# Finished projection chains scaled by ScalarE and added by GpSimd in place of VectorE, in a one-core attention and Fourier kernel

## The chip, the core and the metric

The kernel runs on one core of a Trainium2 chip. The core has a matmul engine (TensorE, "PE" in the profile; its weight loads stand apart as "PEld"), VectorE ("DVE"), ScalarE ("ACT"), GpSimd ("POOL") and SyncE ("SP"), which here only issues DMAs. Each engine takes its instructions from a queue of its own, in the order in which the program wrote them. The metric is the device time of one execution in microseconds (us); lower is better.

## The reference

```
g = sigmoid(sum(x * gate_w))                       # one gate per row
a = Real(DFT_seq(DFT_hid(x)))                      # Cr @ (x @ Wr) - Ci @ (x @ Wi)
qkv = x @ wqkv ; 32 heads of 16                    # attention over the same x
p = softmax(q @ k^T / 4)
b = (p @ v, heads side by side) @ wo
out = g * a + (1 - g) * b                          # 2048 x 512, fp32
```

There are 2048 rows and 512 columns. All products that need more accuracy are split into a high and a low part and taken three times (high x high, high x low, low x high).

## The kernel before, in words

**Stages.** First come the projections to q, k and v, the imaginary half of the hidden DFT and the gate. The long middle part runs attention and, woven into it, the Fourier products. Its unit of work is a "unit": one pair of heads, one key tile of 128, and a half (1024) of the queries. There are 16 pairs x 32 units = 512 (`UNITS`). Each unit has four score products (`scores`, L721, exponentiated by ScalarE in L722 into `pt`) and its value products (`pv`, L757). The maxima that the softmax needs are made ahead from a second set of score products (`a_tile`, L222), which VectorE reduces (L224). When the maxima of half of a head pair are complete, `m_parts` (VectorE L233, GpSimd L236 and L237) and `m_rows` (VectorE L241, then four DMAs from SP and four from GpSimd, L245) write them as two extra rows into the query stack `qs`; SP writes those of head 0, GpSimd those of head 1. The scores of that half read them.

**Sections.** `segment` writes one section by hand: score products on one half of TensorE's rows, products of some accumulating chain on the other, and at the bar `|` the value products of two units. Two sections make a pair that handles the upper and lower halves of the contraction for the same chain products. The pattern `FULL` carries 16 chain products (the Fourier chains over the sequence), the pattern `NINE` carries nine, which is one whole chain of the output projection:

```
NINE = "aS s a s a sA a a s a s sA |", "aS a s s a sA a s a s s aS sA |"
for gen, n in ((proj(1, (0, 1, 2), one), 8), (first, 6)):
    for i in range(n):
        yield NINE, take(gen, 9)
```

So there are 14 pairs of `NINE` sections, for row tiles 8 to 15 and then 0 to 5. They begin at value step 432 and end at step 488. The chain (`Chain`) lies in a PSUM bank of its own (`psD`, tile name `d`). The scores, maxima and value products share the seven other banks, each taken by `bank`, which picks the one that its clocks expect to be free first.

**The end of a section.** At the bar, `segment` writes in this order: the finishes of chains that ended there (`late`, which calls `proj_next` and `finish`), then `add_sums` (the GpSimd add L772 of the value products of the section before, whose copy `oe` ScalarE made in L766 into one of two buffers; the first group of a half is copied straight into `osum`, L763), then `run_plan` (work that falls due at a value step), then the value products of this section, then one deferred step of the maxima.

**Due at the end.** `run_plan` puts the last column block of the attention output into step 486 (`last_block` step 0: two GpSimd memsets L533 and twelve loads by SP, L539 and L540, into `o_raw`), into step 490 (the GpSimd product L574) and into step 494 (VectorE, L562 and L563). Behind step 488 come eleven steps written out in `whole`, in which the last chains run on all rows of TensorE, and then the last pair of heads (`LastPair`, `last_pair`).

**A finish.** `finish` adds `(1 - g)` times a chain to the row tile `yp[t]`. Its VectorE form is one instruction (L596). It also has a form with ScalarE and GpSimd (L593, L594), which only three finishes at the very end use, with the tile `few` for the scaled chain.

Of the kernel before, what the change touches and what calls it, by code (L numbers as in the profile page):

```python
# [9 lines left out]
F32 = mybir.dt.float32  # L10
# [5 lines left out]
P = 128  # L16
S = 2048
D = 512
# [5 lines left out]
UNITS = NP * 32  # L24
# [7 lines left out]
def mix_kernel(ctx: ExitStack, tc: tile.TileContext, xa_t, xa, wqkv, w_hid, w_seq, wo, gate_w, out):  # L32
# [317 lines left out]
    work = ctx.enter_context(tc.tile_pool(name="work", bufs=1, side="right", reuse_waits="tile"))  # L350
# [134 lines left out]
    oh, yp, wos = {}, {}, []  # L485
# [101 lines left out]
    few, by_others = [], set()  # L587

    def finish(ps, t, y, other=False):
        if other:  # L590

            tmp = few[0][:, t % 4]
            nc.scalar.activation(tmp, ps, AF.Copy, scale=omg[:, t:t + 1])  # L593
            nc.gpsimd.tensor_tensor(y, y, tmp, ALU.add)  # L594
            return
        nc.vector.scalar_tensor_tensor(y, ps, omg[:, t:t + 1], y, op0=ALU.mult, op1=ALU.add)  # L596

    def proj(hf, cts, pools):

        for qt in range(8):  # L600
            t = hf * 8 + qt
            chain = Chain(pools[qt % len(pools)], 3 * len(cts))
            for ct in cts:
                h1, l1 = oh[hf, ct][qt]
                for i, (st, mv) in enumerate(((h1, 0), (h1, 1), (l1, 0))):
                    last = ct == cts[-1] and i == 2
                    yield chain, st, wos[0][:, mv, ct], partial(proj_next, hf, cts, t, chain) if last else None

    def proj_next(hf, cts, t, chain):
        finish(chain.ps, t, yp[t], t in by_others)  # L610
        if hf == 0 and cts[-1] == 3:
            nc.sync.dma_start(out[t * P:(t + 1) * P, :], yp[t])

# [23 lines left out]
    class LastPair:  # L637
# [31 lines left out]
        def products(self, others):  # L669

            pss = [o_bank() for _ in range(4)]
            for i, (st, mv) in enumerate(((0, 0), (0, 1), (1, 0))):
                for c in range(4):
                    r = slice(32 * c, 32 * c + 32)
                    nc.tensor.matmul(pss[c], self.o15[r, st], w15[0][r, mv], start=i == 0, stop=i == 2)  # L675
            for c in range(4):
                t = 8 + 4 * self.blk + c
                y = yp.pop(t)
                finish(pss[c], t, y, c in others)
                nc.sync.dma_start(out[t * P:(t + 1) * P, :], y)  # L680
# [185 lines left out]
    users, valued = [], 0  # L866
# [159 lines left out]
```

## Time and profile before

| what | us |
|---|---|
| median of 3 runs (lowest, highest) | 1688.51 (1687.78, 1689.23) |
| the profiled execution | 1688.01 |
| its span on the core | 1686.2 |
| busy: PE, DVE, ACT, POOL | 1674.4, 1370.7, 1246.6, 747.8 |
| one finish on VectorE (L596), median of those from bank `d` | 0.74 |
| one scaling on ScalarE (L593) / one add on GpSimd (L594) | 0.69 / 1.27 |

Matmuls are pipelined and their ends are modelled, so a PE that is busy all the time still has waits inside; they show as idle time ahead of a weight load (PEld), with the engine that ended it. In a timeline row stand the start, the time, the engine, the source line, the operation, the tiles (out<-in), the shape, the count, and in brackets the idle time of that engine before it and what ended it. "SPq" is SyncE's DMA queue.

### The profile page before, as it was taken

The numbers are of one execution on the slowest core, as the hardware profiler recorded it, in microseconds if no ns is written. First come the engines' busy times: TensorE is split into PE (matmuls) and PEld (weight loads), VectorE is DVE, ScalarE is ACT, GpSimd is POOL, SyncE is SP. The second block draws the span as 40 slices with busy tenths as digits, with TensorE's granted clock in tenths as the row PEclk, the third lists the DMA queues.
The fourth block names the chain that finished last, engine by engine and source line by source line (L and its number), as shares of the span: only waits on it lengthen the run. The fifth ranks groups of instructions, "written<-read, shape, count | busy, mean of one in ns | idle before, by whom it ended". The sixth has DMA issues, their size and how long they took to land.

```text
span 1686.2 us, 34488 instructions
## 1 busy us (share of the span) xinstructions
PE 1674.4 (99%) x13072; PEld 1016.5 (60%) x13072; DVE 1370.7 (81%) x2283; ACT 1246.6 (74%) x2472; POOL 747.8 (44%) x807
## 2 busy tenths in 40 slices
PE   9999999999999999999999999999999999999998
PEld 7888766655555555555555555555555555565643
DVE  5448688888888888888888888888888888899944
ACT  5212288887777888777777788778777888787896
POOL 0114634554444465444444466445554465322230
PEclk9999999999999999999999999999999999999999
DMA  9963500314141533314155533332241536740114
GB/s 295 340 151 114 174 10 21 45 51 77 44 83 46 102 97 83 70 46 95 45 132 189 103 121 86 86 68 60 70 89 46 112 96 129 263 70 8 33 27 139
DMA packets 82486, 165.15 MB, mean 98 GB/s; under 512 B 19777, under 2 KB 20033, under 8 KB 78481
## 3 DMA queue, kind: packets, MB, share of 16 engines
q1 hardware_dynamic: 77968, 162.56, 37.3%
q8 instruction: 103, 1.69, 0.5%
q0 software_dynamic: 4352, 0.39, 0.3%
q14 instruction: 63, 0.51, 0.1%
HBM read 107.73 MB, written 54.52 MB: 96 GB/s over the span
## 4 chain that ended last, share of the span: by engine, by line
PE 98%; POOL 1%; DMA 0%; issue 0%; DVE 0%; ACT 0%; DVEq 0%; POOLq 0%; ACTq 0%
PE d L416 38%; PE t L757 27%; PE t L222 12%; PE t L721 8%; PE t L315 4%; PE t L89 2%; PE t L90 2%; PE t L88 2%; PE t L333 1%; PE t L738 1%; PE t L416 0%; DMA raw<-wqkv 0%; POOL hl L292 0%; PE t L675 0%; DMA b<-hl 0%
## 5 line engine op out<-in xcount | busy, mean ns | idle before, releaser
L224 DVE TENSOR_REDUCE mx<-t 128x1 f32<-128x512 f32 x2022 | 1253.9, 683 | 197.6 <-PE t L222 153.1
L722 ACT ACTIVATE pt<-t 128x512 f32<-128x512 f32 x2048 | 1035.1, 629 | 9.5 <-PE t L721 9.3
L721 PE MATMUL t<-qs,ks 50*128 50x512 f32 x2048 | 737.5, 411 | 0.6 <-ACT y L432 0.5
L222 PE MATMUL t<-ks,qs 48*128 48x512 f32 x2022 | 689.9, 400 | 0.0
L416 PE MATMUL d<-xab,ch 64*128 64x512 f32 x2016 | 656.9, 400 | 0.0
L757 PE MATMUL t<-pt,vt 128*32 128x512 f32 x3968 | 477.5, 598 | 0.0
L416 PEld LDWEIGHTS d<-xab,ch 64*128 64x128 f32 x2016 | 357.8, 184 | 132.5 <-issue 99.8
L222 PEld LDWEIGHTS t<-ks,qs 48*128 48x128 f32 x2022 | 366.4, 185 | 91.1 <-ACT pt L722 37.4
L721 PEld LDWEIGHTS t<-qs,ks 50*128 50x128 f32 x2048 | 366.8, 185 | 75.3 <-DVE mx L224 34.9
L416 PE MATMUL d<-xab,cl 64*128 64x512 f32 x1008 | 403.8, 401 | 0.0
L772 POOL TENSOR_TENSOR osum<-osum,oe 128x512 f32<-128x512 f32 x217 | 280.1, 1291 | 164.8 <-ACT oe L766 157.4
L766 ACT COPY oe<-t 128x512 f32<-128x512 f32 x217 | 127.7, 589 | 236.1 <-PE t L757 234.3
L757 PEld LDWEIGHTS t<-pt,vt 128*32 128x32 f32 x3968 | 105.0, 109 | 229.6 <-issue 148.7
L371 POOL CAST ch<-craw 128x512 fp32r<-128x512 f32 x126 | 77.4, 615 | 349.8 <-PE t L721 305.2
L416 PEld LDWEIGHTS d<-xab,cl 64*128 64x128 f32 x1008 | 185.7, 184 | 68.2 <-issue 51.1
L372 POOL TENSOR_TENSOR cl<-craw,ch 128x512 fp32r<-128x512 f32 x126 | 162.6, 1290 | 10.2
L245 POOL DMA_DIRECT2D qs<-mt x128 | 72.3, 570 | 81.9 <-DVE mt L241 75.3
L416 PE MATMUL d<-wo_hl,o_hl 64*128 64x512 f32 (+1 forms) x270 | 72.6, 392 | 0.8 <-DVE yp_qs L596 0.8
L416 PE MATMUL d<-wre,xab 64*128 64x512 f32 x288 | 70.4, 389 | 0.0
L416 PEld LDWEIGHTS d<-wre,xab 64*128 64x128 f32 x288 | 52.9, 185 | 3.8 <-DVE mx L224 0.3
L416 PEld LDWEIGHTS d<-wo_hl,o_hl 64*128 64x128 f32 (+1 forms) x270 | 49.5, 185 | 4.8 <-DVE yp_qs L596 1.3
L89 PE MATMUL t<-xab,wh 128*128 128x512 f32 x128 | 49.9, 390 | 0.2 <-DVE xab L85 0.2
(121 smaller groups left out, 893.3 us busy)
## 6 DMA issues: line engine op xcount, KB each, us to landing
craw<-w_seq SPq DMA_DIRECT2D x128, 256.0 KB
qk<-hl SPq DMA_DIRECT2D x32, 512.0 KB
qs<-qk SPq DMA_DIRECT2D x96, 128.0 KB
ks<-qk SPq DMA_DIRECT2D x96, 128.0 KB
b<-hl SPq DMA_DIRECT2D x16, 512.0 KB
xab<-b SPq DMA_DIRECT2D x16, 512.0 KB
o<-osum SPq DMA_DIRECT2D x62, 128.0 KB
oh<-nh SPq DMA_DIRECT2D x12, 512.0 KB
```

The lines of the kernel that those rows point to most:

```text
L89: nc.tensor.matmul(ps, sh, ml, start=False, stop=False)
L222: nc.tensor.matmul(ps, qs[p % 2][r, qt * P:(qt + 1) * P], ks[p % 2][r, kb * 512:(kb + 1) * 512], start=True, stop=True)
L224: user = nc.vector.tensor_reduce(mx[p % 2][:, h, qt, kb:kb + 1], ps, AX.X, ALU.max)
L245: (nc.sync, nc.gpsimd)[h].dma_start(rows.rearrange("v (q b c) -> v b q c", q=8, b=4)[:, b], mt[hf][32 * b + h:32 * b + 32:2])
L371: nc.gpsimd.tensor_copy(h1, raw)
L372: nc.gpsimd.tensor_tensor(l1, raw, h1.bitcast(F32), ALU.subtract)
L416: i = nc.tensor.matmul(self.ps, st[r], mv[r], start=not self.begun, stop=stop)
L721: nc.tensor.matmul(ps, ks[p % 2][rr, kt * P:(kt + 1) * P], qs[p % 2][rr, q0:q0 + 512], start=True, stop=True)
L722: return nc.scalar.activation(pts[u][:, 2 * qb + h], ps, AF.Exp, bias=0.0, scale=DH ** -0.5)
L757: nc.tensor.matmul(acc[32 * j:32 * j + 32], vt[:, kt, p, h:h + 32], pt[:, j], start=u == us[0], stop=u == us[-1])
L766: nc.scalar.copy(oe, acc)
L772: nc.gpsimd.tensor_tensor(o, o, oe, ALU.add)
```

## The change

In all 14 pairs of `NINE` sections, `finish` takes its second form: ScalarE scales the chain out of its bank into a tile in SBUF, and GpSimd adds that tile to the row tile. The condition `valued < UNITS - 24` is true for every value step below 488. The tile `few` does not exist yet at that time, so the scaled chain goes into two tiles of the working pool in turn, `nh` for even row tiles and `no` for odd ones. Both served the column blocks of the attention output before and are used again at step 494. Finishes behind step 488 stay as they were. The patterns of the sections and the choice of the banks are not touched.

```
     def finish(ps, t, y, other=False):
         if other:
-            tmp = few[0][:, t % 4]
+            tmp = few[0][:, t % 4] if few else work.tile([P, 2, D], F32, name="no" if t % 2 else "nh")[:, 0]
             nc.scalar.activation(tmp, ps, AF.Copy, scale=omg[:, t:t + 1])
             nc.gpsimd.tensor_tensor(y, y, tmp, ALU.add)
             return
         nc.vector.scalar_tensor_tensor(y, ps, omg[:, t:t + 1], y, op0=ALU.mult, op1=ALU.add)
...
     def proj_next(hf, cts, t, chain):
-        finish(chain.ps, t, yp[t], t in by_others)
+        finish(chain.ps, t, yp[t], t in by_others or valued < UNITS - 24)
         if hf == 0 and cts[-1] == 3:
             nc.sync.dma_start(out[t * P:(t + 1) * P, :], yp[t])
```

More of the change, by code (lines that the diff above doesn't have):

```diff
@@ L590, in finish @@
         if other:
-            tmp = few[0][:, t % 4]
+            tmp = few[0][:, t % 4] if few else work.tile([P, 2, D], F32, name="no" if t % 2 else "nh")[:, 0]
             nc.scalar.activation(tmp, ps, AF.Copy, scale=omg[:, t:t + 1])
@@ L609, in proj_next @@
     def proj_next(hf, cts, t, chain):
-        finish(chain.ps, t, yp[t], t in by_others)
+        finish(chain.ps, t, yp[t], t in by_others or valued < UNITS - 24)
         if hf == 0 and cts[-1] == 3:
```

## The prediction, made before the changed kernel ran

> **What bounds the kernel now.** I read the page, then the windows of the stage that the change touches, then the timeline of each engine there and after it.
>
> ```profile
> PE 1674.4 (99%) x13072; PEld 1016.5 (60%) x13072; DVE 1370.7 (81%) x2283; ACT 1246.6 (74%) x2472; POOL 747.8 (44%) x807
> ...
> core 0: us, PE busy (x) PEld busy (x) DVE busy (x) ACT busy (x) POOL busy (x), PEclk, DMA share, GB/s
> 1513.70:1525.00 11.30, 11.30 (x86) 6.63 (x82) 10.40 (x19) 9.03 (x18) 2.58 (x2) 1.00 0.21 79
> ```
>
> TensorE never goes empty, and the sections with nine products ("nine sections") come in pairs of 11.30 us. In one pair VectorE works 10.40, ScalarE 9.03, GpSimd 2.58. So VectorE looks nearly full, and whether taking 0.74 from it helps depends on where that 0.74 lies. This is one pair end, in order of time (the all-engine timeline):
>
> ```profile
> 1508.36 0.18 PEld L222 LDWEIGHTS t<-ks,qs 48*128 48x128 f32 x1 [0.84 <-DVE mx L224]
> 1508.89 4.88 DVE L224 TENSOR_REDUCE mx<-t 128x1 f32<-128x512 f32 x8 [0.47 <-PE t L721]
> 1508.98 4.52 ACT L722 ACTIVATE pt<-t 128x512 f32<-128x512 f32 x9
> 1512.45 1.92 PE L757 MATMUL t<-pt,vt 128*32 128x512 f32 x16
> 1513.68 0.74 DVE L596 SCALAR_TENSOR_TENSOR yp<-d,omg,yp 128x512 f32<-128x512 f32 x1
> 1514.30 0.18 PEld L222 LDWEIGHTS t<-ks,qs 48*128 48x128 f32 x1 [0.84 <-DVE mx L224]
> 1514.48 0.18 PEld L416 LDWEIGHTS d<-wo_hl,o_hl 64*128 64x128 f32 x1
> 1514.52 0.59 ACT L766 COPY oe<-t 128x512 f32<-128x512 f32 x1 [1.02 <-PE t L757]
> 1514.84 4.88 DVE L224 TENSOR_REDUCE mx<-t 128x1 f32<-128x512 f32 x8 [0.42 <-PE t L721]
> ```
>
> While TensorE does the value products (from 1512.45) it hands VectorE nothing new. The finish (L596) runs there, and afterwards VectorE is still idle for 0.42 us until TensorE's next score. In the half without a finish (1508.89) that idle time is 0.47, and the restart of TensorE shows the same 0.84 at 1508.36 and 1514.30. So the finish is hidden already: its removal lengthens an idle stretch and is worth 0.
>
> **The change, part by part.** 14 finishes lie in the nine sections (8 of the second half's rows, 6 of the first's). Each loses one VectorE instruction of 0.74 and gains a ScalarE scaling and a GpSimd add. TensorE's instructions keep their order, and the choice among the seven banks is what it was.
>
> *ScalarE.* The same form already runs once, at the end of a long chain just ahead of these sections (timelines of ScalarE and GpSimd):
>
> ```profile
> 1452.16 0.59 ACT L766 COPY oe<-t 128x512 f32<-128x512 f32 x1 [1.29 <-PE t L757]
> 1452.64 4.03 ACT L722 ACTIVATE pt<-t 128x512 f32<-128x512 f32 x8
> 1456.56 0.69 ACT L472 ACTIVATE y<-d,ng 128x512 f32<-128x512 f32 x1
> 1457.97 0.59 ACT L766 COPY oe<-t 128x512 f32<-128x512 f32 x1 [0.72 <-PE t L757]
> 1457.32 1.29 POOL L473 TENSOR_TENSOR y<-y,yr 128x512 f32<-128x512 f32 x1 [8.94 <-ACT y L472]
> 1458.56 2.66 POOL L772 TENSOR_TENSOR osum<-osum,oe 128x512 f32<-128x512 f32 x2
> ```
>
> A scaling of 0.69 between the exponentials and the copy of the value products shrank ScalarE's idle time from 1.29 to 0.72 and moved nothing else. In a nine section it has 1.02 to fit into, so about 0.4 is left: cost 0. Without that cover it would be 14 x 0.69 = 9.7. Queued behind it on ScalarE is only that copy. The bank of the chain comes free at 1508.98 + 4.52 + 0.6 = 1514.1, not at 1514.42, and TensorE loads for its next use at 1514.48: no gain there either, since the matmuls beside it set that time.
>
> *GpSimd.* 14 adds of 1.29 (L473) on an engine that is busy 2.58 of 11.30: room enough. What changes is its order. The queue is in program order, the add of a finish is put ahead of the add of the first half's value products (L772), and it waits for ScalarE's end of the section. So that L772, which ran at once, runs up to 6 us later. In most pairs nobody needs it: it is done by 1514.1 + 0.07 + 1.24 + 1.29 = 1516.7, and its buffer (one of two) is wanted by the copy of the next section's products, a half pair of 5.35 after 1514.52, at 1519.9. The last pair differs, because more hangs behind it in the same queue:
>
> ```profile
> 1611.04 1.30 POOL L772 TENSOR_TENSOR osum<-osum,oe 128x512 f32<-128x512 f32 x1 [4.10 <-ACT oe L766]
> 1612.25 1.87 POOL L533 MEMSET o_raw<- 128x1024 f32 x2
> 1615.38 0.20 POOL L236 CAST nhl<-nm 128x16 fp32r<-128x16 f32 x1 [1.26 <-DVE nm L233]
> 1622.79 2.38 POOL L574 TENSOR_TENSOR o_raw<-o_raw 128x1024 f32<-128x1024 f32 x1 [4.83 <-DMA o_raw<-r]
> 1625.11 2.31 POOL L245 DMA_DIRECT2D qs<-mt  x4
> 1627.44 3.07 POOL L772 TENSOR_TENSOR osum<-osum,oe 128x512 f32<-128x512 f32 x2
> ...
> 1613.26 0.51 SPq L539 DMA_DIRECT2D o_raw<-o  x1
> ...
> 1620.39 0.59 SPq L540 DMA_DIRECT2D o_raw<-r  x1
> 1621.08 2.75 SPq L245 DMA_DIRECT2D qs<-mt  x4
> ```
>
> The memsets (L533) gate twelve loads that SP issues without a pause from 1613.26 to 1621; behind these stand SP's four writes of the maxima rows (L245); GpSimd's L574 waits for the last load, and GpSimd's own four L245 wait behind L574. In the changed order the add of row tile 5 stands ahead of L772 and the memsets. When does it run?
>
> ```profile
> 1610.80 4.52 ACT L722 ACTIVATE pt<-t 128x512 f32<-128x512 f32 x9
> 1616.02 0.59 ACT L766 COPY oe<-t 128x512 f32<-128x512 f32 x1 [0.70 <-PE t L757]
> ...
> 1632.53 0.59 ACT L766 COPY oe<-t 128x512 f32<-128x512 f32 x1
> 1633.01 4.03 ACT L722 ACTIVATE pt<-t 128x512 f32<-128x512 f32 x8
> ...
> 1632.34 1.82 PE L721 MATMUL t<-qs,ks 50*128 50x512 f32 x8
> 1634.16 1.92 PE L757 MATMUL t<-pt,vt 128*32 128x512 f32 x16
> ...
> DMA to landing us min/median/max: 1.7/1.7/2.1
> ```
>
> The exponentials end at 1615.32. L472 began 0.11 before its group's end, so the scaling runs 1615.21 to 1615.90 and the copy at 1616.02 is not moved. The add follows 0.07 later (1457.25 to 1457.32): 1615.97. One such add passes to the next in 1.24 (1457.32 to 1458.56), L772 to the memset in 1.21 (1611.04 to 1612.25): the memset starts at 1618.42 in place of 1612.25, **6.17 late**. Everything in the two queues that I named moves by this: SP's L245 end at 1623.83 + 6.17 = 1630.0, GpSimd's last L245 is issued at 1627.42 - 0.58 + 6.17 = 1633.0, and with 1.7 to landing its rows are there at 1634.7.
>
> Who needs them: the scores of the last 16 units, which read these rows; the first are the eight at 1632.34. SP writes head 0's rows (1630.0 + 1.7 = 1631.7: in time, by 0.6), GpSimd head 1's, needed by the second matmul at about 1632.5. Before, they were there at 1628.5, with 4.0 to spare; so TensorE now waits 6.17 - 4.0 = **2.2** (2.8 if the landing counts from the issue's end). ScalarE is stopped too: the copy at 1632.53 needs the buffer that the first of the two L772 at 1627.44 reads. It ends after half of 3.07, at 1628.98, now 1635.15: the copy comes **2.6** late, and the exponentials of 1633.01 with it. Both stops cover the same time, so the end moves by about 2.4, the smaller one with a little of the other; TensorE and ScalarE run on without slack to give it back. Ends for this term: 0 (if the 4.0 is larger than I read it) and 4 (each landing 2.1 and the later casts of VectorE, 6.17 late as well, in the way).
>
> Sum: finishes 0, scalings 0, adds 0, last pair +2.4. The profiled execution took 1688.01 (span 1686.2 and 1.8 around it): 1690.4. The median of the runs shown, 1688.51, is 0.5 above that execution: **1690.9**. That is +0.14%; 0.2%, about what a measurement of this kernel tells from no change, is 3.4 us.
>
> **The rivals.** *VectorE was the bound (faster).* If TensorE's restart waited for the finish, each pair would lose the 0.60 by which the half with a finish is longer (1508.89 to 1514.84 is 5.95, against 5.35 without: 1503.54 to 1508.89):
>
> ```profile
> 1503.54 4.88 DVE L224 TENSOR_REDUCE mx<-t 128x1 f32<-128x512 f32 x8 [0.43 <-PE t L222]
> ```
>
> 14 x 0.60 = 8.4 less, with the last pair 1688.5 - 8.4 + 2.4 = 1682.5. For it: VectorE is busy 92% of a pair. Against it: the 0.42 of idle time behind the finish, ended by TensorE; and that half has nine exponentials and one slot more. [...] Chance 0.06.
>
> *ScalarE becomes late (slower).* If the scaling's wait or its length pushes the copy of the value products past TensorE's end, the next section's exponentials and the banks that they free are late in each pair. It decides from 1.02 - 0.69 = 0.33 of further delay on; at full price 14 x 0.69 = 9.7: 1688.5 + 9.7 + 2.4 = 1700.6. Against it: L472's row. Chance 0.06.
>
> *The adds' length matters.* GpSimd's 1.29 and the 0.69 ahead of it replace 0.74: 14 x 1.24 = 17.4 if each finish were waited for, 1705.9. The row tiles are touched again only tens of us later, so 0.01. [...]
>
> *The last pair hides it.* The rows land in time: 1688.5, chance 0.09. That no finish is moved at all is excluded: the condition holds for every value step below 488, and the nine sections end there.
>
> *The last pair costs more than 3.4.* Price 4, 1692.5; from a landing or a cast about 1 us later than computed. Chance 0.16.
>
> **How the numbers follow.** My forecast (1.5 to 3.5 more) has 0.62. Faster by over 0.2%: 0.06. Slower: 0.06 + 0.01 + 0.16 + 0.02 of the forecast's upper edge = 0.25. Within: 0.69. The range leaves out the two engine rivals and the adds' (0.13) and little more: from the hidden case with the runs' spread, 1688.0, to the dear last pair with it, 1693.0.
>
> **What would show it.** Right: pairs still 11.30; L593 behind the nine exponentials with some 0.4 of idle time before L766; the memset near 1618.4, L574 near 1629; the eight scores near 1632.3 stretched by over 2 us, waiting for a DMA, and the copy beside them for GpSimd. Wrong: pairs shorter (VectorE was the bound) or longer (ScalarE late); the memset where it was; the rows late with no stop of TensorE; or a new stop somewhere that I called covered.

## The result, and the profile after

| kernel | median, us | lowest to highest | runs |
|---|---|---|---|
| before | 1688.51 | 1687.78 to 1689.23 | 7 |
| after | 1692.75 | 1690.45 to 1694.03 | 7 |

The ratio is 1.0026, with a 95% interval of 1.0016 to 1.0035: the change makes the kernel slower by some 0.26%. The medians differ by 4.24 us; the forecast was 2.4 us slower. The profiled execution of after took 1693.67 (span 1691.9, mean granted clock 0.997), that of before 1688.01 (span 1686.2, clock 0.999). Of the 5.7 between the two spans some 0.4 arises ahead of the first moved finish (the value products just before it start at 1467.63 and not at 1467.22). At the end of the last pair this shift is still 0.38 (1613.99 and 1613.61). So the change has to explain 5.3 in this pair of executions.

The page and the windows of two pairs, as before (columns: us, then busy time and count of each engine, granted clock, DMA share, GB/s):

```profile
PE 1678.2 (99%) x13072; PEld 1015.1 (60%) x13072; DVE 1361.2 (80%) x2269; ACT 1254.9 (74%) x2486; POOL 763.8 (45%) x821
...
core 0: us, PE busy (x) PEld busy (x) DVE busy (x) ACT busy (x) POOL busy (x), PEclk, DMA share, GB/s
1513.70:1525.00 11.30, 11.30 (x86) 6.56 (x82) 9.74 (x17) 9.55 (x20) 2.52 (x2) 1.00 0.24 89
1536.30:1547.60 11.30, 11.30 (x86) 6.58 (x82) 9.75 (x17) 9.60 (x20) 3.81 (x3) 1.00 0.01 1
```

VectorE lost its 0.66 per pair (10.40 to 9.74) and ScalarE gained 0.52 (9.03 to 9.55). The pairs got neither shorter nor longer: between the two executions the shift is 0.41 ahead of the 14 finishes and 0.38 at the last one. One pair end, from the timelines of VectorE, ScalarE and GpSimd:

```profile
1515.24 4.87 DVE L224 TENSOR_REDUCE mx<-t 128x1 f32<-128x512 f32 x8 [1.08 <-PE t L721]
...
1513.69 0.78 ACT L593 ACTIVATE nh<-d,omg 128x512 f32<-128x512 f32 x1
1514.93 0.59 ACT L766 COPY oe<-t 128x512 f32<-128x512 f32 x1 [0.45 <-PE t L757]
...
1514.55 1.28 POOL L594 TENSOR_TENSOR yp<-yp,nh 128x512 f32<-128x512 f32 x1 [7.35 <-ACT nh L593]
1515.79 1.28 POOL L772 TENSOR_TENSOR osum<-osum,oe 128x512 f32<-128x512 f32 x1
```

VectorE's idle time ahead of the next score grew from 0.42 to 1.08, by the 0.66 that it lost: the finish had been hidden. ScalarE's scaling took 0.78 and not 0.69, and still left 0.45 idle ahead of the copy. The add L772 now stands behind the add of the finish, and here nobody waits for it.

The last pair is where the time went. From the timelines of GpSimd, SP's queue, TensorE and ScalarE:

```profile
1616.35 1.29 POOL L594 TENSOR_TENSOR yp_qs<-yp_qs,no 128x512 f32<-128x512 f32 x1 [8.83 <-ACT no L593]
1617.58 1.30 POOL L772 TENSOR_TENSOR osum<-osum,oe 128x512 f32<-128x512 f32 x1
1618.80 1.87 POOL L533 MEMSET o_raw<- 128x1024 f32 x2
...
1629.52 2.39 POOL L574 TENSOR_TENSOR o_raw<-o_raw 128x1024 f32<-128x1024 f32 x1 [7.17 <-DMA qs<-mt]
1631.85 2.29 POOL L245 DMA_DIRECT2D qs<-mt  x4
...
1619.81 0.51 SPq L539 DMA_DIRECT2D o_raw<-o  x1
...
1632.76 0.50 PE L721 MATMUL t<-qs,ks 50*128 50x512 f32 x1
1635.42 2.08 PE L721 MATMUL t<-qs,ks 50*128 50x512 f32 x7 [2.17 <-DMA qs<-mt]
1637.43 3.64 PE L757 MATMUL t<-pt,vt 128*32 128x512 f32 x16
...
1635.57 0.59 ACT L766 COPY oe<-t 128x512 f32<-128x512 f32 x1 [2.74 <-POOL osum L772]
```

Read it downwards: the add of row tile 5 waits 8.83 for ScalarE, the memsets start at 1618.80 (1612.25 before: 6.55 later, of which 0.38 is the later start, so 6.17), SP's first load at 1619.81, GpSimd's four DMAs of the maxima rows at 1631.85; TensorE has done one score and stands still for 2.17. So far it is the chain of the prediction. (The idle time of L574 is put down there to a DMA of the maxima rows; in the kernel with the filled stop below the same row names `o_raw<-r`, which is what the product reads.) But the value products behind it (L757) take 3.64 for sixteen, and 1.92 before. The windows of TensorE alone tell why (columns: us, PE busy, granted clock, DMA share, GB/s):

```profile
1633.00:1634.00 1.00, 0.25 (x1) 1.00 0.06 5
1634.00:1635.00 1.00, 0.00 (x0) 1.00 0.06 5
1635.00:1636.00 1.00, 0.58 (x5) 1.00 0.00 0
1636.00:1637.00 1.00, 1.00 (x5) 0.53 0.00 0
1637.00:1638.00 1.00, 1.00 (x6) 0.50 0.00 0
...
1642.00:1643.00 1.00, 1.00 (x4) 0.55 0.03 8
1643.00:1644.00 1.00, 1.00 (x5) 1.00 0.00 0
```

Some 0.65 us after TensorE has resumed, its granted clock falls to 0.50 and stays there for 6.8 us, from about 1636.07 to 1642.9 (the 0.53 and 0.55 place the two ends). In before the clock is 1.00 in every window from 1630 to 1680, two of which are:

```profile
1636.00:1637.00 1.00, 1.00 (x9) 1.00 0.00 0
...
1642.00:1643.00 1.00, 1.00 (x6) 1.00 0.00 0
```

Groups of TensorE from 1630 to 1690, first of before, then of after (busy us, mean ns of one | idle ahead):

```profile
L721 PE MATMUL t<-qs,ks 50*128 50x512 f32 x68 | 13.2, 446 | 0.0
L757 PE MATMUL t<-pt,vt 128*32 128x512 f32 x32 | 3.8, 598 | 0.0
```

```profile
L721 PE MATMUL t<-qs,ks 50*128 50x512 f32 x68 | 14.3, 474 | 2.2 <-DMA qs<-mt 2.2
L757 PE MATMUL t<-pt,vt 128*32 128x512 f32 x32 | 5.6, 829 | 0.0
```

The stop is 2.2; the same matmuls behind it take 1.1 and 1.8 longer. Together 5.1 of the 5.3. This execution is one of the dearer ones; the one run of after whose mean clock is 0.999 took 1690.45 (span 1688.7, 2.5 above that of before), and the six with 0.996 or 0.997 took 1692.07 to 1694.03. A stretch of 6.8 us at half clock takes 3.4 / 1691 = 0.002 off a mean clock, which is the step from 0.999 to 0.997.

### The profile page after: what moved, and what is told of

Read it like the earlier page. It is cut to its first block, busy times and chain, and to the rows that moved or that the text cites. A ratio compares the mean times of both kernels' runs of the same rounds, so it can differ in the third digit from the quotient of the medians.

```text
span 1691.9 us, 34506 instructions
## 1 busy us (share of the span) xinstructions
PE 1678.2 (99%) x13072; PEld 1015.1 (60%) x13072; DVE 1361.2 (80%) x2269; ACT 1254.9 (74%) x2486; POOL 763.8 (45%) x821
## 4 chain that ended last, share of the span: by engine, by line
PE 98%; POOL 1%; issue 0%; DMA 0%; DVE 0%; ACT 0%; DVEq 0%; POOLq 0%; ACTq 0%
PE d L416 39%; PE t L757 27%; PE t L222 12%; PE t L721 8%; PE t L315 4%; PE t L88 2%; PE t L89 2%; PE t L90 2%; PE t L333 1%; PE t L738 1%; PE t L416 0%; PE t L159 0%; POOL hl L292 0%; PE t L675 0%; DMA b<-hl 0%
## 5 line engine op out<-in xcount | busy, mean ns | idle before, releaser
L757 PE MATMUL t<-pt,vt 128*32 128x512 f32 x3968 | 479.2, 600 | 0.0
L772 POOL TENSOR_TENSOR osum<-osum,oe 128x512 f32<-128x512 f32 x217 | 279.7, 1289 | 71.7 <-ACT oe L766 68.9
L757 PEld LDWEIGHTS t<-pt,vt 128*32 128x32 f32 x3968 | 105.1, 109 | 230.6 <-issue 149.5
L245 POOL DMA_DIRECT2D qs<-mt x128 | 72.0, 568 | 75.2 <-DVE mt L241 72.6
```

The lines of the kernel that those rows point to most:

```text
L245: (nc.sync, nc.gpsimd)[h].dma_start(rows.rearrange("v (q b c) -> v b q c", q=8, b=4)[:, b], mt[hf][32 * b + h:32 * b + 32:2])
L757: nc.tensor.matmul(acc[32 * j:32 * j + 32], vt[:, kt, p, h:h + 32], pt[:, j], start=u == us[0], stop=u == us[-1])
L772: nc.gpsimd.tensor_tensor(o, o, oe, ALU.add)
```

## The experiments

Three accounts were to be told apart. The first is that everything comes from the last pair: the stop by the late rows costs 2.4, as forecast, and the clock that falls behind the stop costs the rest. The second is that the fourteen moved finishes each cost something (ScalarE's or GpSimd's added work) and the last pair is only a part. The third is that the moved finish itself, by its reads and writes, slows what runs beside it. A fourth question was whether VectorE's freed time is worth anything once the stop is gone. The first four kernels were compared with 30 runs of before on the same chip: 1688.65 (1687.98 to 1689.45).

**Thirteen finishes moved, the last one left on VectorE.**

```
-        finish(chain.ps, t, yp[t], t in by_others or valued < UNITS - 24)
+        finish(chain.ps, t, yp[t], t in by_others or valued < UNITS - 26)
```

> The changed kernel, but the finish of the last nine section (row tile 5) stays on VectorE; the other 13 stay on ScalarE and GpSimd. Theory Q (the queue: that one add stands ahead of the memsets in GpSimd's queue, and all of the loss follows from it): the memset is back near 1612, TensorE does not stop at the scores of unit 496, and the time is that of the kernel before, 1688.5 (within 0.1%). Rival S (each of the 14 moved finishes costs a little on ScalarE or in contention): 13/14 of the loss stays, 1692.4.

Measured: 1688.74 (1688.30 to 1689.17, 11 runs), ratio 1.0000 (0.9991 to 1.0009); every run has the mean clock 0.999. GpSimd's memsets stand at their old place (but for the start of this execution), and TensorE's eight scores are one group again, with no stop:

```profile
1612.95 1.86 POOL L533 MEMSET o_raw<- 128x1024 f32 x2
...
1633.08 1.82 PE L721 MATMUL t<-qs,ks 50*128 50x512 f32 x8
```

Thirteen finishes off VectorE, thirteen scalings on ScalarE and thirteen adds on GpSimd are worth nothing in either direction that the interval (some 1.5 us each way) shows. The second account is gone.

**Only the last finish moved.**

```
+        finish(chain.ps, t, yp[t], t in by_others or valued == UNITS - 26)
```

> The kernel before with only the finish of row tile 5 moved to ScalarE and GpSimd. Theory Q: the whole loss is there, 1692.5 in most runs, with the stop of about 2.2 us ahead of the second score of unit 496. Rival S: 1/14 of the loss, 1688.8.

Measured: 1692.82 (1692.01 to 1694.22, 8 runs), ratio 1.0027 (1.0017 to 1.0038). One finish of fourteen brings the whole loss. The profiled execution has the stop, and no lowered clock: the sixteen value products take their 1.92. Its run took 1692.12, and the two runs with a mean clock of 0.999 are the two lowest of the eight.

```profile
1619.33 1.86 POOL L533 MEMSET o_raw<- 128x1024 f32 x2
...
1635.87 1.77 PE L721 MATMUL t<-qs,ks 50*128 50x512 f32 x7 [2.10 <-DMA qs<-mt]
1637.64 1.92 PE L757 MATMUL t<-pt,vt 128*32 128x512 f32 x16
```

So, by the mean clocks (0.999 in two of the eight runs, 0.996 or 0.997 in five, 0.998 in one), it falls behind the stop in some executions of this program and not in others. These lowest runs are above the 1690.45 of after. A part of it is a later start (the first score, at 1633.27, is 0.93 later than in before, of which the stop is no part yet), and another is time outside the span, 2.1 where before and after have 1.8. Most of the later start stands ahead of the moved finish, where the two kernels do not differ (the copy of the value products at 1452.16 in before is at 1453.05 here), so it is not the work of the change; what makes it, and the 2.1, is not explained. That the medians 1692.82 and 1692.75 agree so closely is therefore in part luck.

**All fourteen moved, but written behind the add of the value products and the planned work.** Same instructions, another place in GpSimd's queue.

```
             if slot == "|":
-                for f in late:
-                    f()
+                if pattern not in NINE:
+                    for f in late:
+                        f()
                 add_sums()
                 run_plan(valued)
+                if pattern in NINE:
+                    for f in late:
+                        f()
                 values()
```

> The changed kernel with all 14 finishes moved, but in a nine section the finish is written behind the add of the value products and behind the work that falls due (the memsets), not ahead of them; no engine has another amount of work. Theory Q: the memset runs near 1612 again, no stop, 1688.5. Rival S: 1692.7 as the changed kernel. If VectorE had been a bound at all, this one would be faster than the kernel before.

Measured: 1689.15 (1688.66 to 1689.71, 11 runs), ratio 1.0003 (0.9994 to 1.0012). The memsets run ahead of the add and on time; the add runs when ScalarE is done, and nobody waits behind it:

```profile
1612.63 1.86 POOL L533 MEMSET o_raw<- 128x1024 f32 x2
...
1616.34 1.29 POOL L594 TENSOR_TENSOR yp_qs<-yp_qs,no 128x512 f32<-128x512 f32 x1 [1.85 <-ACT no L593]
```

It is the place in the queue that costs, not the work. And the fourth question is answered too: with all fourteen finishes off VectorE and no stop, the kernel is no faster than before (the 0.5 above it is within the interval, and 0.4 of it lies outside the span: 2.2 there, against 1.8, for no reason that the runs show).

**After, with the stop filled.** Behind the first score of unit 496, TensorE gets eight matmuls into the bank that is due next; their results are not used.

```
             for h in range(2):
                 scores(u + i // 2, i % 2, h)
+                if u == 496 and i == 0 and h == 0:
+                    ps = banks[min(range(7), key=lambda j: free[j])].tile([P, 512], F32, name="t")
+                    for _ in range(8):
+                        nc.tensor.matmul(ps, oh[0, 0][0][0], wos[0][:, 0, 0], start=True, stop=True)
```

> The changed kernel with eight extra matmuls (results unused) between the first and the second score of unit 496, where TensorE stops for 2.2 us; they take about that long. The profile of the changed kernel shows TensorE's granted clock at 0.5 from about 1636 to 1642.5 after the stop. Theory C (the stop itself costs 2.4, and the rest of the loss is the lowered clock that it sets off): no lowered clock, mean granted clock 0.999 in all runs, time 1690.9. Rival N (the rest comes from ScalarE's stop or elsewhere, the clock only tells of it): 1692.7 as the changed kernel, or more.

Measured: 1690.98 (1690.55 to 1691.85, 11 runs), ratio 1.0014 (1.0005 to 1.0023); every run has the mean clock 0.999. The eight fill the stop almost exactly, the second score still comes when its row is there, and what follows runs at full speed:

```profile
1632.54 0.50 PE L721 MATMUL t<-qs,ks 50*128 50x512 f32 x1
1632.97 2.11 PE L983 MATMUL t<-wo_hl,o_hl 128*128 128x512 f32 x8
1635.14 1.68 PE L721 MATMUL t<-qs,ks 50*128 50x512 f32 x7
1636.81 1.92 PE L757 MATMUL t<-pt,vt 128*32 128x512 f32 x16
```

```profile
1637.00:1639.00 2.00, 2.00 (x18) 1.00 0.00 0
1639.00:1641.00 2.00, 2.00 (x12) 1.00 0.02 4
```

Work that adds nothing to the result makes after 1.8 us faster (1692.75 to 1690.98; 1.9 if each is taken against its own runs of before, 1688.51 and 1688.65). What is left, 1690.98 - 1688.65 = 2.33, is the price of the late rows by themselves; the forecast had 2.4.

**Before, with idle memsets in GpSimd's queue.** The last three kernels move no finish. Ahead of the memsets L533 they put five, six or eight memsets of a tile that nobody reads, so the rows come late by a known amount. They ask where the cover ends (how late the rows may be before TensorE has to wait), and whether a stop lowers the clock without the moved finish. They were compared with 21 runs of before: 1688.51 (1687.68 to 1689.21).

```
             t = last_o[0][:, hf]
+            if n < 4:
+                idle = work.tile([P, 2, D], F32, name="no")
+                for _ in range(5):            # 6 and 8 in the other two
+                    nc.gpsimd.memset(idle, 0.0)
             load_o(t[:, 0], t[:, 1], hf, 3, 0, n)
```

> The kernel before, all finishes on VectorE, with five unneeded GpSimd memsets (each like one of the two L533, which pass in some 0.9 us) ahead of the two that gate the loads. No finish is moved; only GpSimd's queue is late. Theory Q: the gating memset is 4.5 late against a cover of 4.0, so TensorE stops for about 0.5; 1689.1, no lowered clock. Rival M (the moved finish itself matters, by its work on ScalarE and GpSimd beside TensorE): 1688.6, as before, here and in the two runs below.

> The same with six: 5.4 late, a stop of 1.4. Theory Q: 1690.0 if the clock holds. Theory C (a stop long enough lowers TensorE's clock for some us): a shorter stop than the changed kernel's 2.2 lowers it seldom or never, so the runs lie close together. Rival M: 1688.6.

> The same with eight: 7.1 late, a stop of 3.1. Theory Q without C: 1691.7. With C: the clock is lowered in every run, for longer than in the changed kernel, and 2 to 3 us come on top, 1694 to 1695. Rival M: 1688.6.

| memsets | median (lowest to highest), runs | ratio (95%) | rows late by | TensorE's stop |
|---|---|---|---|---|
| 5 | 1690.67 (1689.23 to 1691.52), 10 | 1.0013 (1.0003 to 1.0022) | 5.0 | 0.70 |
| 6 | 1692.13 (1690.42 to 1693.55), 10 | 1.0020 (1.0010 to 1.0030) | 6.0 | 1.68 |
| 8 | 1693.96 (1693.38 to 1694.98), 6 | 1.0033 (1.0021 to 1.0045) | 8.0 | 3.16 and 0.54 |

In each kernel's timeline of GpSimd the idle memsets give the lateness (1.0 for each memset), and rows of TensorE give the stops. The four inserted lines shift the numbers of the lines behind them: here L574 is the idle memset, L725 the scores and L770 ScalarE's copy.

```profile
1612.50 5.01 POOL L574 MEMSET no<- 128x1024 f32 x5
...
1630.21 2.31 POOL L245 DMA_DIRECT2D qs<-mt  x4
...
1633.78 1.80 PE L725 MATMUL t<-qs,ks 50*128 50x512 f32 x7 [0.70 <-DMA qs<-mt]
```

```profile
1612.42 6.03 POOL L574 MEMSET no<- 128x1024 f32 x6
...
1631.15 2.30 POOL L245 DMA_DIRECT2D qs<-mt  x4
...
1634.71 1.79 PE L725 MATMUL t<-qs,ks 50*128 50x512 f32 x7 [1.68 <-DMA qs<-mt]
```

```profile
1612.37 8.05 POOL L574 MEMSET no<- 128x1024 f32 x8
...
1633.09 0.47 PE L725 MATMUL t<-qs,ks 50*128 50x512 f32 x1 [0.54 <-DMA qs<-mt]
1636.72 2.05 PE L725 MATMUL t<-qs,ks 50*128 50x512 f32 x7 [3.16 <-DMA qs<-mt]
```

Lateness less stop is 4.3 in each of the first two, but 4.0 in after (6.17 less 2.17). The difference arises between the memsets and the rows: counted at GpSimd's four DMAs of the maxima rows (L245), the three agree. These DMAs start 7.23 ahead of the first score in before, and 2.37 ahead of it with five memsets (first score at 1632.58), 1.39 with six (1632.54) and 0.91 in after. So they are 4.86, 5.84 and 6.32 later, and less the stop that is 4.16, 4.16 and 4.15. The cover is about 4.15 us, where the prediction had 4.0.

Without any moved finish, six memsets (6.0 late) cost 3.6 where the change costs 4.2 (6.17 late), with intervals that overlap. Together with the 13 moved finishes that cost nothing, this leaves nothing for the third account to explain.

The eight-memset kernel shows the clock fall too, this time inside the stop:

```profile
1634.00:1636.00 2.00, 0.00 (x0) 0.70 0.04 4
1636.00:1638.00 2.00, 1.28 (x6) 0.50 0.06 9
1638.00:1640.00 2.00, 2.00 (x11) 0.50 0.00 0
1640.00:1642.00 2.00, 2.00 (x14) 0.59 0.00 0
1642.00:1644.00 2.00, 2.00 (x14) 1.00 0.00 0
```

The lowered stretch runs from about 1634.8 to 1641.6, 6.8 us again, but its first 1.9 us fall on time in which TensorE waits anyway. So the fall costs less here: ScalarE's copy waits 4.3 in this kernel, and 1693.96 is 5.45 above before, which leaves some 1.2 for the clock (an estimate, if that wait is the price of the stop), against 1.8 in after.

Three things came out otherwise than the expectations had them. The clock was expected to fall seldom or never behind a stop shorter than that of after. With six memsets three of ten runs have a mean clock of 0.997, which no run without a stop has, and four have 0.998; these seven took 1691.18 to 1693.55, and the three with 0.999 took 1690.42 to 1690.68. With five the ten runs fall into two groups, five from 1689.23 to 1690.19 and five from 1691.15 to 1691.52; the profiled one is of the first group and keeps its clock, so that the second group's 1.5 more is the clock's work is argued from that alone and not shown: its mean clock is 0.998 in all five, but two runs of the first group and some of before have 0.998 as well, and a stop of 0.70 is far shorter than the stops of 2.17 (after) and 3.16 (eight memsets) at which the traces show a fall. The second is the eight-memset kernel: its lowered stretch was expected to be longer than that of after and to cost 2 to 3 us, and it is as long and costs less. The third is the price without the fall: the three 0.999 runs of the six-memset kernel lie 2 above before with a stop of TensorE of 1.68. There ScalarE's copy waits 2.25 for its buffer (1.3 with five), longer than TensorE's stop, and this seems to set the price; no run takes one stop away and leaves the other.

## Why the prediction was right or wrong

**Finishes off VectorE, 0: right.** VectorE's idle time behind a finish grew by what was removed, and 13 finishes moved give 1688.74 against 1688.65. The rival that VectorE was the bound falls, although VectorE was busy 92% of a pair.

**Scalings on ScalarE, 0: right,** with 0.78 each in place of 0.69; 0.45 of idle time was left, as forecast (0.4).

**Adds on GpSimd, 0 but for the last: right.** Their length did not matter; their place did.

**Last pair: the chain was right and the term mis-sized, 2.4 for 4.2.** The memset 6.17 late came out to the hundredth, the stop of TensorE at the second score as 2.17 (2.2), ScalarE's copy as 2.74 (2.6), and the price of these stops as 2.33 (2.4). That the first two fit so closely is luck: the scaling began 0.10 earlier than computed and took 0.09 longer, and GpSimd's DMAs of the rows were 6.32 late against a cover of 4.15, where the prediction had 6.17 and 4.0. The step that failed is "TensorE and ScalarE run on without slack to give it back": they did, but TensorE not at its former speed. In the profiled run its granted clock fell to 0.50 for 6.8 us behind the stop, and the mean clocks (0.996 or 0.997) tell of the same in six of the seven runs; it was worth 1.8 in the median (1692.75 less 1690.98). So the forecast's main case, 1.5 to 3.5 more, did not come. The case "the last pair costs more than 3.4", with a price of 4, is what came, for another reason than it gave: the landings took 1.7 / 1.9 / 2.9 (lowest, median, highest) in place of 1.7 / 1.7 / 2.1, but the stop was as long as computed. The prediction took the 1.00 that before's windows show for a constant, and no row that it used showed what TensorE does behind a stop. Had the clock been counted as these runs show it, that case would have been the likeliest. Before's own trace has one fall, to 0.50 at 1681.67, some 2.7 us behind the end of the last matmul (1678.94), where nothing waits for TensorE any more; the prediction did not look there.

## What to carry to other kernels

An engine that is busy 92% of a stage may still be off the path: look for its idle time directly behind the instruction to be moved (here 0.42 us) before counting on it. When an instruction that waits for another engine is put into an in-order queue, read on in that queue to the next thing that gates a DMA; here one add of 1.29 us ahead of two memsets cost all that was lost, and writing it behind them cost nothing that the interval shows (1689.15 against 1688.65). And a stop of TensorE is not priced by its length alone: see what clock it gets afterwards (here 0.50 for 6.8 us, behind a stop of 2.17), and if the stop can't be avoided, filler matmuls may be cheaper than an idle array (here eight of them were worth 1.8 us).

## What the runs showed of the hardware

TensorE's granted clock fell to 0.50 some 0.65 us behind a stop of only 2.17 us, and with eight idle memsets some 1.2 us into a stop of 3.16. It stayed there for 6.8 us in both of these executions. By the mean clocks it fell in six of seven runs of after (0.996 or 0.997) and in none of eleven where eight matmuls filled the stop (0.999 in each).

In the profiled executions of before and after the clock also falls to 0.50 some 2.7 us behind the end of the last matmul: at 1681.67 (last matmul to 1678.94) and at 1687.27 (to 1684.60). At the stop of the last pair the clock held behind 2.10 (only the last finish moved), 1.68 (six memsets) and 0.70 (five) in the profiled executions. So 2.10 passed in one execution and 2.17 was followed by a fall in another, and by the mean clocks the kernel with only the last finish moved does both. What decides in which execution the clock falls is not shown: no experiment moved a stop in time at the same length, and of the runs without a trace only the mean clock is known.

Two versions of the same change without the stop (the last finish on VectorE; all finishes written behind the planned work) come out level with before, and none beats it.
